# Output stage of a linear-attention block: numerators three output products ahead instead of four, and each residual add ahead of the division

## Chip, cores, metric

The kernel runs on one core of a Trainium2 chip. The metric is device time in microseconds (us), the median of several runs. All runs compared here are of the fast state; e11 is a single run, whose state is unknown, and serves for its profile alone. The kernel before takes 736.35 us (median of 6 runs, 735.11 to 737.95).

## The reference, cut to what matters

```
h  = x + attn(layernorm(x))          # S = 2048 tokens, D = 1024, 32 heads
h2 = h + reglu_mlp(layernorm(h))
# attn, after q, k, v and phi:
num = pq @ kv;  den = pq @ z + 1e-6
o = num / den                        # per token and head
attn = o @ wo
```

The change concerns the last two lines: the numerators, the division, the product with `wo` and the residual add, for 16 tiles of 128 tokens.

## The kernel before

Every operation is added to one plan with the buffers that it reads and writes. Each engine, and SyncE's DMA queue, works through its own list strictly in order. The functions of the output stage, cut to what matters:

```python
def a2_num(st):                      # N(st): 32 small matmuls into PSUM banks 0 to 3
    ...
def a2_div(st):                      # D(st): +1e-6, reciprocal, multiply, on VectorE
    ...
    dma_t(sl_to[kt], oT[:, kt, :, :], osb[:, k, :], ...)      # X(st): DMA transpose on SyncE's queue
def a4_mm(st):                       # O(st): 2 x 8 matmuls into a pair of banks (4,5 or 6,7)
    k = st % NOT                     # NOT = 4
    ...
def a4_h(st):                        # H(st): residual add on VectorE, frees the pair of banks
    ...
    if TPP <= st and st + NX2 < NST: # from tile 8 on: load x of tile st + 3
        load_x2(st + NX2)
    dma(sl_hs[hs], h_scr[...], hsb[:, hs, :], ...)            # W(st): store
    if st >= TPP: return
    ...                              # statistics of the second layer norm on ScalarE, GpSimd
def a4_norm(st):                     # L(st), then its DMA transpose Y(st), tiles 0 to 7
    ...
    dma_t(sl_tx[kx], hnT[...], xn[:, kx, :], ...)
```

The loop before (N, D and X of tiles 0 to 3 are done earlier, among the q products):

```python
LAG = NOT                            # 4
for t in range(NE, NST + LAG + 1):   # NE = 4
    if LAG <= t < NST + LAG:
        a4_mm(t - LAG)
    if t < NST:
        a2_num(t)
        a2_div(t)
    if LAG <= t < NST + LAG:
        a4_h(t - LAG)
    if LAG + 1 <= t < TPP + LAG + 1:
        a4_norm(t - LAG - 1)
    if t in (5, 7, 18, 19):
        load_w_next()                # 512 KB of feed-forward weights each
    ...                              # sums of weights on GpSimd, sums of tokens on VectorE
```

## Time and profile before

| | us |
|---|---|
| span of the profiled run | 734.9 |
| TensorE busy | 720.8 (98%) |
| from the end of O(0) to the end of O(15) | 57.6 |
| after O(15) | 503.7 |
| one step of the stage on TensorE: O 3.63, N 0.23 | 3.86 |

TensorE hardly ever waits, so the time is read from its waits and from what is about to become one. A line of the timeline gives start, length, engine, line of the kernel, operation, output<-input, and in brackets the idle time in front and what ended it. In names, RE<-RE is X, RH<-RXH is Y, h_scr<-RXH is W, RWG<-in_B_W_gate_dram and RWG<-in_B_W_up_dram are the weight loads; matmuls from RW,RE are O and from kvz,RAB are N.

### The profile page before, as it was taken

The page shows a single profiled execution, that of the slowest core. Times are in us where ns is not written, and L with a number is a line of the kernel's source. Part 1 is how long each engine was busy: PE and PEld are TensorE (multiplying, and loading weights), DVE is VectorE, ACT ScalarE, POOL GpSimd, SP SyncE. Part 2 cuts the span into 40 slices and gives each one's busy share as a digit, 9 for nine tenths or more (in the row PEclk, how much of TensorE's full clock was granted, in tenths as well). Part 3 has the DMA queues.
Part 4 walks back from the last instruction along what each step waited for, and adds up shares of the span by engine and source line. Part 5 has one row for each costly group of instructions (what it writes and reads, how often), then busy time and mean ns, then how long its engine had stood idle before and what let it go on. Part 6 is the DMA issues. An engine that isn't in the chain of part 4 may idle for free.

```text
span 734.9 us, 11505 instructions
## 1 busy us (share of the span) xinstructions
PE 720.8 (98%) x4253; PEld 363.2 (49%) x4311; DVE 561.6 (76%) x976; ACT 352.0 (48%) x614; POOL 103.7 (14%) x169
## 2 busy tenths in 40 slices
PE   8999999999999999999999999999999999999998
PEld 3444444344444444444444666754444444447766
DVE  7878877898775999898997769865757575667594
ACT  4877666764832456777754100135454544521000
POOL 1311100000450112132320003400000000000052
PEclk9999999999999999999999999999999999999999
DMA  9644154024999889888969999982323242327892
GB/s 313 202 91 83 29 142 157 3 30 75 214 228 260 234 258 272 241 243 256 300 198 305 318 247 336 311 263 79 101 71 109 63 116 58 100 92 245 246 314 87
DMA packets 191880, 133.93 MB, mean 182 GB/s; under 512 B 51664, under 2 KB 173776, under 8 KB 191824
## 3 DMA queue, kind: packets, MB, share of 16 engines
q1 hardware_dynamic: 191152, 132.54, 63.6%
q8 instruction: 34, 0.56, 0.3%
q10 hardware_dynamic: 672, 0.66, 0.3%
q14 instruction: 22, 0.18, 0.1%
HBM read 96.47 MB, written 25.17 MB: 166 GB/s over the span
## 4 chain that ended last, share of the span: by engine, by line
PE 82%; DVE 9%; DMA 3%; issue 2%; ACT 2%; SPq 1%; POOL 1%; POOLq 0%; DVEq 0%; ACTq 0%
PE ps L710 82%; DMA RW<-in_B_W_down_dram 1%; DVE RAB L796 1%; DVE RE L1171 1%; ACT RX L789 1%; DMA RX<-h_scr 1%; DVE st L724 1%; DMA RAB<-RXH 1%; DVE RX L793 1%; SPq L541 1%; DVE RX L1012 1%; DVE RO L1289 1%; POOL rstd L734 0%; DVE RW L906 0%; ACT ps L715 0%
## 5 line engine op out<-in xcount | busy, mean ns | idle before, releaser
L715 ACT ACTIVATE ps<-ps 128x512 f32<-128x512 f32 x172 | 100.1, 582 | 213.5 <-PE ps L710 162.0
L710 PE MATMUL ps<-RC,RO 128*128 128x512 f16 x672 | 154.3, 379 | 0.0
L710 PE MATMUL ps<-RH,RWG 128*128 128x512 bf16 x447 | 105.6, 379 | 0.1
L710 PEld LDWEIGHTS ps<-RC,RO 128*128 128x128 f16 x672 | 65.7, 98 | 79.5 <-ACT ps L715 0.5
L1345 DVE TENSOR_TENSOR RAB<-ps,RAB 128x512 bf16<-128x512 f32 x56 | 38.6, 689 | 71.9 <-PE ps L710 71.9
L710 PE MATMUL ps<-RC,RWG 128*128 128x512 f16 x320 | 76.8, 379 | 0.3 <-ACT ps L715 0.3
L1341 DVE TENSOR_TENSOR RE<-ps,RE 128x512 bf16<-128x512 f32 x112 | 74.2, 684 | 1.6 <-PE ps L710 0.7
L710 PEld LDWEIGHTS ps<-RH,RWG 128*128 128x128 bf16 x448 | 43.9, 98 | 52.6
L710 PE MATMUL ps<-RW,RAB 128*128 128x256 f16 (+3 forms) x412 | 66.8, 318 | 1.5 <-DVE RAB L1423 1.0
L1423 POOL TENSOR_TENSOR RE<-RE,RX 128x512 f32<-128x512 f32 x16 | 23.1, 1473 | 307.5 <-DMA RX<-h_scr 307.5
L715 ACT ACTIVATE RE<-RE 128x512 bf16<-128x512 bf16 x56 | 35.1, 627 | 65.0 <-DVE RE L1341 64.4
L710 PE MATMUL ps<-RH,RO 128*128 128x512 bf16 (+1 forms) x228 | 55.3, 379 | 3.0 <-DVE RE L1341 1.6
L710 PE MATMUL ps<-RW,RE 128*128 128x512 bf16 x243 | 56.6, 380 | 1.5 <-DVE RXH L1195 0.7
L710 PE MATMUL ps<-RAB 128*128 128x512 bf16 (+2 forms) x268 | 57.6, 351 | 0.4
L715 ACT ACTIVATE RE<-ps 128x512 f32<-128x512 f32 x64 | 37.6, 597 | 35.4 <-PE ps L710 35.0
L710 PEld LDWEIGHTS ps<-RW,RAB 128*128 128x128 bf16 (+1 forms) x414 | 40.4, 98 | 25.8 <-DVE RAB L1423 1.3
L710 PEld LDWEIGHTS ps<-RC,RWG 128*128 128x128 bf16 (+1 forms) x320 | 30.0, 98 | 40.2 <-ACT ps L715 6.2
L1289 DVE TENSOR_TENSOR RO<-RWG 128x1024 f16<-128x1024 bf16 x54 | 39.7, 736 | 4.7 <-DMA RWG<-in_B_W_up_dram 4.7
L1423 DVE TENSOR_TENSOR RE<-ps,RE 128x512 f32<-128x512 f32 x40 | 27.0, 687 | 18.9 <-PE ps L710 15.6
L715 ACT ACTIVATE RAB<-ps 128x512 bf16<-128x512 f32 x56 | 33.4, 596 | 14.7 <-PE ps L710 13.6
L710 PEld LDWEIGHTS ps<-RH,RO 128*128 128x128 f16 (+1 forms) x256 | 24.2, 98 | 31.8 <-DVE RE L1341 2.2
L710 PEld LDWEIGHTS ps<-RAB 128*128 128x128 bf16 (+1 forms) x274 | 26.3, 98 | 25.2 <-ACT RAB L856 1.1
(138 smaller groups left out, 994.0 us busy)
## 6 DMA issues: line engine op xcount, KB each, us to landing
RWG<-in_B_W_gate_dram SPq DMA_DIRECT2D x28, 512.0 KB, 5.0
RWG<-in_B_W_up_dram SPq DMA_DIRECT2D x28, 512.0 KB, 5.9
RW<-in_B_W_down_dram SPq DMA_DIRECT2D x14, 512.0 KB, 6.1
t_scr<-RW SPq DMA_DIRECT2D x14, 512.0 KB, 3.5
RE<-in_A_x_dram SPq DMA_DIRECT2D x23, 256.0 KB, 3.5
RW<-l_scr SPq DMA_DIRECT2D x13, 448.0 KB, 6.3
l_scr<-RX SPq DMA_DIRECT2D x7, 768.0 KB, 4.4
RW<-in_B_W_down_dram SPq DMA_DIRECT2D x12, 384.0 KB, 5.0
```

The costliest lines, as they stand in the source:

```text
L541: return PL.add(eng, lambda e: e.dma_start(dst_ap, src_ap), reads=reads, writes=writes, slot=slot, name=name)
L710: lambda e: e.matmul(out_ap, lhsT, rhs, start=start, stop=stop, skip_group_check=skip),
L715: PL.add("act", lambda e: e.activation(out=dst, in_=src, func=func), reads=reads, writes=writes, name=name)
L724: PL.add("dve", lambda e: e.bn_stats(out=st6[:, k, c * 6:(c + 1) * 6], in_=src_full[:, c * BCH:(c + 1) * BCH]), reads=[src_chunk_bufs[c]], ...
L789: PL.add("act", lambda e: e.activation(out=Et[:, k, :], in_=src, func=ACTF.Exp), reads=[src_buf], writes=[B_E[k]], name=name + "_exp")
L793: PL.add("dve", lambda e: e.tensor_scalar(out=Et[:, k, :], in0=Et[:, k, :], scalar1=1.0, scalar2=1e-6, op0=ALU.min, op1=ALU.add), reads=[] ...
L796: PL.add("dve", lambda e: e.scalar_tensor_tensor(out=dst_ap, in0=src, scalar=C1, in1=Et[:, k, :], op0=ALU.add, op1=ALU.max), reads=[src_bu ...
L1012: PL.add("dve", lambda e: e.tensor_tensor(out=s_, in0=p_, in1=s_, op=ALU.add), reads=[pb], writes=[sb_], name=name + "_add")
L1289: PL.add(eng, lambda e: e.tensor_tensor(out=tb(j, u), in0=f0(u), in1=f1(u), op=ALU.subtract), reads=[B_w[i + x] for x in r] + ([B_T[k + x] ...
L1341: PL.add("dve", lambda e: e.tensor_tensor(out=dst, in0=src, in1=ftmp[:, w, :], op=ALU.add), reads=[bsrc, B_s5[w]], writes=[bdst], name=name)
L1345: PL.add("dve", lambda e: e.tensor_tensor(out=dst, in0=a_, in1=b_, op=ALU.mult), reads=reads, writes=[wr], name=name)
L1423: PL.add(eng, lambda e: e.tensor_tensor(out=dst, in0=in0, in1=in1, op=op), reads=reads, writes=writes, name=name)
```

## The change

Its intent: D(4) kept VectorE from H(0), and O(2) waited for the banks that H(0) frees. The add goes ahead of the division in every step, and the numerators run three products ahead, so that no N stands between O(1) and O(2).

```diff
-        LAG = NOT
+        LEAD = 3
 ...
+        for t in range(NST + 1):
+            if t < NST:
+                a4_mm(t)
+                if t == 0:
+                    a2_num(NE)
+                    a4_h(0)
+                    a2_div(NE)
+                else:
+                    if t + LEAD > NE:
+                        if t + LEAD < NST:
+                            a2_num(t + LEAD)
+                        a4_h(t)
+                        if t + LEAD < NST:
+                            a2_div(t + LEAD)
+                    else:
+                        a4_h(t)
+            if 1 <= t <= TPP:
+                a4_norm(t - 1)
-            if t in (5, 7, 18, 19):
+            if t in (1, 3, 14, 15):
                 load_w_next()
 ...             # the other shifts by four are renamings: same place relative to O
```

More of the change, by code (lines that the diff above doesn't have):

```diff
@@ L1871, in bass_sequential_preLN__linear_attn_block__glu_gated_reglu__prompt_kernel, with a2 @@
         flush()
-        LAG = NOT
         pool_t = t_sums(0, "pool")
-        for t in range(NE, NST + LAG + 1):
-            if LAG <= t < NST + LAG:
-                a4_mm(t - LAG)
+        LEAD = 3
+        def a2(t):
             if t < NST:
@@ L1879, in bass_sequential_preLN__linear_attn_block__glu_gated_reglu__prompt_kernel @@
                 a2_div(t)
-            if LAG <= t < NST + LAG:
-                a4_h(t - LAG)
-            if LAG + 1 <= t < TPP + LAG + 1:
-                a4_norm(t - LAG - 1)
-            if t in (5, 7, 18, 19):
+        for t in range(NST + 1):
[17 more added lines that the diff above has]
+            if t in (1, 3, 14, 15):
                 load_w_next()
-            if t >= 9:
+            if t >= 5:
                 run(pool_t, 1)
-            if 15 <= t < 19:
-                s_sums()[t - 15]()
+            if 11 <= t < 15:
+                s_sums()[t - 11]()
+        run(pool_t, len(pool_t))
         load_w_next()
```

## The prediction

> **Names.** The output stage handles 16 token tiles. N(s) are the 32 numerator products of tile s, D(s) its division on VectorE (three instructions, lines 1166, 1169, 1171), X(s) the DMA transpose that puts the divided tile before TensorE, O(s) the 16 matmuls of the output product, H(s) the residual add (line 1195), W(s) the store of H(s), L(s) the second layer norm on ScalarE, Y(s) its DMA transpose (tiles 0 to 7 only). X, W, Y and all loads are issued by one queue, SyncE's, in program order.
>
> **What bounds the kernel now.** I read the page first: busy shares, then the chain of work that ended last.
>
> ```profile
> PE 720.8 (98%) x4253; PEld 363.2 (49%) x4311; DVE 561.6 (76%) x976; ACT 352.0 (48%) x614; POOL 103.7 (14%) x169
> ...
> PE 82%; DVE 9%; DMA 3%; issue 2%; ACT 2%; SPq 1%; POOL 1%; POOLq 0%; DVEq 0%; ACTq 0%
> ```
>
> TensorE is busy 720.8 of 734.9 us. So whatever the stage gains is time in which TensorE waits, and anything that makes it wait is added to the end. Next, the waits of TensorE: 1.6 us on line 1341, 1.4 on line 522, 1.0 on line 1423, and in the stage concerned one single wait of 0.7 us on H (line 1195). The timeline shows where it lies:
>
> ```profile
> 173.84 3.63 PE L710 MATMUL ps<-RW,RE 128*128 128x512 bf16 x15
> ...
> 176.06 1.23 DVE L1171 TENSOR_TENSOR RE<-ps,rden 128x1024 bf16<-128x1024 f32 x1
> 177.20 1.21 DVE L1195 TENSOR_TENSOR RXH<-ps,RC 128x1024 bf16<-128x1024 f32 x1
> 177.40 0.27 PEld L710 LDWEIGHTS ps<-kvz,RAB 32*128 32x128 bf16 x32 [0.42 <-DVE RE L1171]
> ...
> 178.47 1.90 PE L710 MATMUL ps<-RW,RE 128*128 128x512 bf16 x7 [0.70 <-DVE RXH L1195]
> ```
>
> O(1) runs at 173.84, N(5) at 177.40, then O(2) needs the two PSUM banks of O(0). H(0) frees them at 178.41, for VectorE did D(4) first. From O(2) on, the timeline has TensorE without a gap worth counting: O(3) starts at 182.33 and each next one 3.86 us later (3.63 for O, 0.23 for N), O(5) at 190.06, O(9) at 205.51, until O(15) ends at 231.17 and the feed-forward stage follows directly.
>
> The view that decides is SyncE's own timeline. Column two is how long the queue was occupied:
>
> ```profile
> 184.94 1.23 SPq L545 DMA_TRANSPOSE RH<-RXH  x1
> 186.21 0.58 SPq L541 DMA_DIRECT2D RWG<-in_B_W_gate_dram  x1
> 186.91 2.21 SPq L545 DMA_TRANSPOSE RE<-RE  x1
> 189.56 0.33 SPq L541 DMA_DIRECT2D h_scr<-RXH  x1
> 189.95 1.37 SPq L545 DMA_TRANSPOSE RH<-RXH  x1
> 191.44 2.07 SPq L545 DMA_TRANSPOSE RE<-RE  x1
> 193.56 0.58 SPq L541 DMA_DIRECT2D h_scr<-RXH  x1
> 194.19 1.29 SPq L545 DMA_TRANSPOSE RH<-RXH  x1
> 195.52 0.61 SPq L541 DMA_DIRECT2D RWG<-in_B_W_up_dram  x1
> 196.24 2.14 SPq L545 DMA_TRANSPOSE RE<-RE  x1
> 198.42 0.58 SPq L541 DMA_DIRECT2D h_scr<-RXH  x1
> 199.04 1.29 SPq L545 DMA_TRANSPOSE RH<-RXH  x1
> 200.45 1.27 SPq L545 DMA_TRANSPOSE RE<-RE  x1
> ```
>
> RE<-RE is X (here X(6) to X(9)), RH<-RXH is Y (Y(0) to Y(3)), h_scr is W. The queue is nearly solid. One tile costs it 3.2 us (1.27 + 0.58 + 1.29 and gaps) to 4.9 us (with a weight load and a 2.1 us X), against 3.86 us of TensorE. D(9) ended at 196.09, yet X(9) is issued at 200.45. Its landing, taken one by one from the view of line 545: X(6) 5.1 us, X(7) 4.1, X(8) 4.9, X(9) 4.8, X(10) 3.9, X(11) 3.1, X(12) 4.4. So X(8) lands at 196.24 + 4.9 = 201.1, and O(8) starts at 201.65; X(9) lands at 205.25, and O(9) starts at 205.51. The four tiles of lead, which look generous, are all used: 0.5 and 0.3 us are left.
>
> **What the Trainium skill says.** (1) "DMA: Bandwidth & Descriptors", section "Anatomy of one DMA": a DMA has a fixed part of about 2.0 us, most of it the receipt of the last write (given there for GpSimd's path), and semaphores are waited for on the issuing sequencer. Section "Latency and other measured facts" of that page has a transpose at 261 GB/s. My estimate from both: 2.0 + 256 KB/261 GB/s = 3.0 us. The trace agrees: X(0), issued with little else about, landed in 3.0 us; 3.1 to 5.1 under load. (2) "Perfetto Trace Analysis", section "What 'DMA-bound' means": a sequencer's track solid with DMA slices is a bound of its own. From 186.9 us on the trace agrees. (3) "VectorE: DVE Perf Modes", the section on the TRN2 errata: an f32 add of N columns takes (N+151)/0.96 ns, 1224 ns for 1024. Line 1195 has 1214 to 1219 ns here, line 1171 1225 ns. (4) "TensorE: Matmul & The Clock Gate", Part 1: the clock halves after an idle window of about 3.4 us. No wait below comes near that, and the mean granted clock here is 1.000.
>
> **The change part by part.** Instruction counts don't change on any engine. Positions of the weight loads, GpSimd sums and S sums relative to O(t) don't change either. Two things do.
>
> *H(0) before D(4).* VectorE is free at 175.4 us. H(0) runs to 176.6, D(4) to 178.5, H(1) from 178.4 to 179.6. O(2) starts straight after O(1), at 177.47. Removed: the 0.70 us wait. D(4) is 1.1 us later; X(4) then lands by about 182 and O(4) wants it at 185.2: beside other work. N(5) moves behind O(2), which costs nothing in sum. Gain 0.7 us.
>
> *Three tiles of lead, add before division in each step.* Per step the queue's order was Y(t-2), X(t+4), W(t), Y(t-1); it becomes W(t), X(t+3), Y(t-1). X(s) thus stands one W more, one Y and in some steps a load further back, 2.5 to 3.1 us. Also D(t+3) waits behind H(t). It ends about 0.1 + 1.13 + 0.23 + 0.46 + 1.23 = 3.2 us after O(t) (the starts of 1195, 1166, 1169, 1171 follow each other so in the trace); now it is 2.4 us.
>
> Step 2, the first with the shorter lead, times from the durations above:
> - O(2) ends at 181.1, D(5) at 184.3.
> - L(0) ended 3.56 us after H(1) (184.92 against 181.36). With H(1) at 179.6 it ends at 183.2. Y(0) goes out there; the next X went out 1.97 us after it (184.94 to 186.91, a weight load between), plus 0.6 for W(2) now between: X(5) at 185.8.
> - It lands after 3.9 us (X(5) before) to 5.1 us (X(6), at this place in the queue): 189.7 to 190.9.
> - O(5) is due at 177.47 + 3 x 3.86 = 189.05. TensorE waits 0.7 to 1.9 us; I take 1.7.
>
> Then, with the waits entered: X(5) holds the queue 2.2 us, Y(1) 1.3, W(3) 0.6: X(6) at 190.0, landed 194.1 to 194.9, O(6) due 194.6: about nothing. X(6) 2.1, Y(2) 1.3, load 0.7, W(4) 0.6: X(7) at 194.7, landed 198.8 to 199.6, O(7) due 198.5: 0.3 to 1.1, I take 0.7. X(7) 2.1, Y(3) 1.3, W(5) 0.7: X(8) at 198.8, landed near 203.4, O(8) due 203.1: 0.3. From there the loop closes over three tiles: O ends, D 3.2 us later, 0.3 to issue, about 4.1 to land, 0.2 to start, 3.63 for O: 11.4 us, against 3 x 3.86 = 11.6. It is in balance, so I give 0.3 us in all for a late landing. Sum: 1.7 + 0.7 + 0.3 + 0.3 = 3.0 us of new waits, less 0.7: the stage 2.3 us longer. All later work starts from O(15)'s end on TensorE, so it shifts by as much.
>
> **Rivals.**
> - *The intended gain and no more.* If X lands in 3.0 to 3.4 us, the wait at O(5) is 0.2 us or less and later ones vanish: 735.5 to 735.8 us. For it: later X land in 3.1 and 3.2 us, and waits of TensorE thin out the DMA load. Against: the measured landings at this place, 3.9 to 5.1.
> - *A longer jam.* X at 4.8 us or more each time: each turn of the loop (11.4 + 0.7) exceeds 11.6 by 0.5 us, some three more turns: 740 us. For it: DMA engines about fully busy from 190 to 226 us. Against: X(10), X(11), X(13) came in 3.9 us or less.
> - *VectorE or the banks become the wait.* H(t) now comes first, so banks come free 2 us sooner; N(t+3) needs D(t+2), done 0.6 us before. Nothing new: about 736.
> - *Clock.* Waits under 2 us leave it at 1.0.
>
> **Range and chances.** 736.2 + 2.3 = 738.5; allowing some weight to the first rival I say 738.0. Low end 735.2 (gain kept, and the runs of before spread over 735.1 to 738.0), high end 740.9 (the jam). 2% is 14.7 us, a quarter of this stage of 61 us: none of this reaches it. Faster 0.005, same 0.985, slower 0.01.
>
> **What would show it.** Right: no wait before O(2); TensorE waits of 0.5 to 2 us for a DMA into RE (X) just before O(5), and one or two smaller ones by O(8); X(5) issued near 185.8; O(15) ending 1 to 4 us later than 231.17. Wrong: O(5) starts at about 189 without a wait (then X landed in 3.2 us or less, or Y(0) left the queue sooner), and O(15) ends near 230.4.

## The result

The changed kernel takes 740.2 us (median of 6 runs, 739.66 to 744.01). Its ratio to before is 1.0069, with a 95% interval from 1.0043 to 1.0095. In a later job it was 740.17 us and 1.0051 (1.0036 to 1.0066). A ratio is the mean time of one kernel's fast runs over that of the other's of the same rounds, so it is not quite the ratio of the medians; the record lists two more fast runs of the changed kernel in that job, 744.70 and 740.93 us, and 1.0069 fits the mean of all eight. The loss is 3.9 us where 1.8 had been predicted.

The page of the changed kernel, first profile, busy shares and chain of work that ended last:

```profile
PE 727.0 (98%) x4311; PEld 364.5 (49%) x4311; DVE 561.7 (76%) x976; ACT 352.0 (47%) x614; POOL 104.1 (14%) x169
...
PE 87%; DMA 4%; DVE 3%; ACT 2%; SPq 1%; issue 1%; POOL 1%; POOLq 0%; ACTq 0%; DVEq 0%
PE ps L710 86%; DMA RE<-RE 2%; DMA RE<-l_scr 1%; DMA RE<-in_A_x_dram 1%; SPq L545 1%; ACT RX L789 1%; DMA RAB<-RXH 1%; POOL RX L1423 1%; DVE RO L1289 1%; SPq L541 1%; ACT ps L715 0%; ACT RXH L748 0%; DMA RX<-h_scr 0%; POOL RE L1423 0%; DVE RAB L1345 0%
```

X (DMA RE<-RE) is now on the chain with 2% of the span. This profile fell on the slowest of the six runs (744.01 us), though: its windows show why it must not be taken for the typical one. The columns are the stretch, its length, each engine's busy time (and instructions), the granted clock, the DMA share and GB/s:

```profile
5.00:10.00 5.00, 2.75 (x15) 1.15 (x14) 3.00 (x8) 0.99 (x2) 1.11 (x2) 0.87 1.07 371
10.00:15.00 5.00, 5.00 (x32) 2.59 (x31) 4.14 (x11) 1.91 (x5) 1.09 (x2) 0.79 1.10 355
```

The clock was low from 5 to 15 us, before anything that was changed; O(0) started 2 us later than in the kernel before. So I took a second profile of the same kernel (run e5 below), with a full clock in that part. What TensorE waited for there, in the order reason: sum in us, times, longest:

```profile
PE ps L710 <- DMA RE<-RE: 4.4, 3, 2.4
PE ps L710 <- POOL RXH L522: 1.4, 1, 1.4
PE ps L710 <- DVE RE L1341: 1.2, 1, 1.2
```

In the first profile the first of these lines reads 5.5 us, also three times. The kernel before has no such line. TensorE's timeline of the second profile shows where:

```profile
173.47 7.08 PE L710 MATMUL ps<-RW,RE 128*128 128x512 bf16 x31
...
190.93 1.37 PE L710 MATMUL ps<-RW,RE 128*128 128x512 bf16 x4 [2.35 <-DMA RE<-RE]
192.53 3.72 PE L710 MATMUL ps<-RW,RE 128*128 128x512 bf16 x11 [0.22 <-issue]
...
201.05 3.63 PE L710 MATMUL ps<-RW,RE 128*128 128x512 bf16 x15 [0.64 <-DMA RE<-RE]
...
221.89 3.40 PE L710 MATMUL ps<-RW,RE 128*128 128x512 bf16 x15 [1.46 <-DMA RE<-RE]
```

The first line is O(1) and O(2) in one: the old wait is gone. O(5), O(7) and O(12) now wait for their transposes. A product has 16 matmuls, and the trace has lost the record of some: where a line of 15 is 3.40 us long instead of 3.63, the first is missing, and the wait in brackets is too long by 0.23 us, here and in the runs below (at O(12) it was 1.23). And O(5), 3.63 us long elsewhere, takes 5.3 us here, for the granted clock (third number from the end) was 0.69 from 190 to 194 us:

```profile
190.00:194.00 4.00, 2.85 (x8) 1.22 (x10) 1.30 (x2) 3.12 (x5) 1.32 (x4) 0.69 1.18 253
194.00:198.00 4.00, 3.95 (x47) 1.67 (x46) 1.62 (x3) 0.34 (x1) 0.00 (x0) 0.89 0.94 229
```

SyncE's queue ahead of those tiles, same profile:

```profile
182.87 1.23 SPq L545 DMA_TRANSPOSE RH<-RXH  x1
184.16 0.57 SPq L541 DMA_DIRECT2D RWG<-in_B_W_gate_dram  x1
184.77 0.64 SPq L541 DMA_DIRECT2D h_scr<-RXH  x1
185.53 1.59 SPq L545 DMA_TRANSPOSE RE<-RE  x1
...
192.71 0.64 SPq L541 DMA_DIRECT2D RWG<-in_B_W_up_dram  x1
193.40 0.63 SPq L541 DMA_DIRECT2D h_scr<-RXH  x1
194.14 2.41 SPq L545 DMA_TRANSPOSE RE<-RE  x1
```

X(5) goes out at 185.53 behind Y(0), a weight load and W(2), X(7) at 194.14 behind the other load and W(4). They land 5.4 and 6.9 us after that (view of line 545, one transpose at a time); X(6) and X(8), with no weight load just in front, land after 3.8 us each.

The stage, from the end of O(0) to the end of O(15), takes 57.6 and 57.7 us in two profiles of before, 64.1 and 62.8 us in the two of the changed kernel.

### The profile page after: what moved, and what is told of

Same layout as the page of the kernel before. It is cut to its first block, busy times and chain, and to the rows that moved or that the text cites. A ratio compares the mean times of both kernels' runs of the same rounds, so it can differ in the third digit from the quotient of the medians.

```text
span 742.3 us, 11564 instructions
## 1 busy us (share of the span) xinstructions
PE 727.0 (98%) x4311; PEld 364.5 (49%) x4311; DVE 561.7 (76%) x976; ACT 352.0 (47%) x614; POOL 104.1 (14%) x169
## 4 chain that ended last, share of the span: by engine, by line
PE 87%; DMA 4%; DVE 3%; ACT 2%; SPq 1%; issue 1%; POOL 1%; POOLq 0%; ACTq 0%; DVEq 0%
PE ps L710 86%; DMA RE<-RE 2%; DMA RE<-l_scr 1%; DMA RE<-in_A_x_dram 1%; SPq L545 1%; ACT RX L789 1%; DMA RAB<-RXH 1%; POOL RX L1423 1%; DVE RO L1289 1%; SPq L541 1%; ACT ps L715 0%; ACT RXH L748 0%; DMA RX<-h_scr 0%; POOL RE L1423 0%; DVE RAB L1345 0%
## 5 line engine op out<-in xcount | busy, mean ns | idle before, releaser
L710 PE MATMUL ps<-RW,RE 128*128 128x512 bf16 x256 | 59.2, 387 | 5.5 <-DMA RE<-RE 5.5
L710 PE MATMUL ps<-RH,RO 128*128 128x512 bf16 (+1 forms) x256 | 61.2, 379 | 1.2 <-DVE RE L1341 1.2
L710 PEld LDWEIGHTS ps<-RW,RE 128*128 128x128 bf16 x256 | 24.5, 99 | 34.7 <-DMA RE<-RE 5.8
```

What stands on the lines that cost most here:

```text
L710: lambda e: e.matmul(out_ap, lhsT, rhs, start=start, stop=stop, skip_group_check=skip),
```

## The experiments

The theory: with a lead of three, X reaches TensorE late, above all behind a weight load in SyncE's queue. Rivals: the residual add ahead of the division delays the division and so X; the mere place at the start of the stage; the clock. "Wait" is TensorE's. All results were correct.

**e1: the first part alone.** Lead four, H(0) ahead of D(4).

```diff
             if t < NST:
                 a2_num(t)
+                if t == NE:
+                    a4_h(t - LAG)
                 a2_div(t)
-            if LAG <= t < NST + LAG:
+            if LAG < t < NST + LAG:
```

> The kernel before with one part of the change alone: H(0) ahead of D(4), lead of four tiles kept. Theory (the loss comes from transposes X that reach TensorE late because the lead is three): no wait of TensorE before O(2), none for X anywhere, 0.7 us faster than before, about 735.6 us. Rival (the residual add ahead of the division delays D and so X): X(4) later by 1.1 us, but it had over 3 us, so no wait here either; this run alone does not refute the rival, it prices the first part.

Measured: 737.26 us, ratio 1.0012 (0.9994 to 1.003). No gain, so the expectation failed. TensorE's timeline:

```profile
178.68 0.37 PE L710 MATMUL ps<-kvz,RAB 32*128 32x33 bf16 x32 [1.13 <-DVE RE L1171]
178.99 3.63 PE L710 MATMUL ps<-RW,RE 128*128 128x512 bf16 x15
```

O(2) starts at 178.99, no sooner than before (178.47). With a lead of four N(5) still stands in front of O(2), and it waits for D(4), which now comes second. The old wait has only changed its name, and O(9) waits 0.3 us more (0.53 in the list, less the 0.23 of a missing record); the list names VectorE, but X(9) landed at 206.5 us, just before O(9) began. The gain needs both parts of the change.

**e2: lead four, add first in every step.**

```diff
             if t < NST:
                 a2_num(t)
-                a2_div(t)
             if LAG <= t < NST + LAG:
                 a4_h(t - LAG)
+            if t < NST:
+                a2_div(t)
```

> Lead of four kept, but in every step the residual add H(t) ahead of the division D(t+4). Theory (lead): X(s) moves back by one store W in the queue, 0.6 us; O(8) and O(9), which had 0.5 and 0.3 us, may wait some tenths; total within 0.7 us of before, 735.5 to 737. Rival (the order of add and division is the cause): most of the loss of 3.9 us appears here, 739 us or more.

Measured: 736.38 us, ratio 0.9999 (0.9982 to 1.0016). Waits: 1.1 us of N(5) for D(4), 0.4 us of O(9) for X(9). As the theory had it; the order of add and division is not what costs 3.9 us.

**e3: lead three, division first from step 2 on.**

```diff
                         if t + LEAD < NST:
                             a2_num(t + LEAD)
-                        a4_h(t)
-                        if t + LEAD < NST:
                             a2_div(t + LEAD)
+                        a4_h(t)
```

> The changed kernel (lead of three) with the division ahead of the residual add again from step 2 on. Theory (lead): X(s) gains only one store W in the queue, 0.6 us, waits at O(5) and O(7) shrink from 2.4 and 1.9 us to about 1.8 and 1.3; 738.5 to 739.5 us. Rival (order): the waits vanish, 735.5 to 736.5 us.

Measured: 741.84 us, ratio 1.0069 (1.0054 to 1.0084). TensorE's wait for X in the list (sum, times, longest):

```profile
PE ps L710 <- DMA RE<-RE: 5.8, 3, 2.6
```

The rival of the order falls, but the theory's number is missed too: waits of 1.4 us at O(5), 2.6 at O(7) and 1.8 at O(12), no smaller in sum than in the changed kernel. X(5) and X(7) had one store fewer in front and still landed in 5.0 and 6.6 us. The stage took 62.6 us, as in the changed kernel (62.8 in e5); that this run is longer lies mostly after O(15), where its profile has a wait of 1.4 us for a load from the scratch tensor `l_scr` that e5 lacks.

**e4: lead three, the two weight loads ahead of the stage.**

```diff
         pool_t = t_sums(0, "pool")
+        load_w_next()
+        load_w_next()
 ...
-            if t in (1, 3, 14, 15):
+            if t in (14, 15):
```

> The changed kernel, with the two weight loads of steps 1 and 3 issued ahead of the output stage instead, so that no 512 KB load stands in the queue before X(5) and X(7). If those loads are what made X(5) and X(7) land in 5.4 and 6.5 us: they land in about 4 us and are issued 0.6 us earlier, the waits fall to about 0.4 us at O(5) and none at O(7), total 736 to 737 us. If the shorter lead is too short whatever the loads do: waits of over 1 us stay at O(5) or later, total 739 us or more.

Measured: 736.53 us, ratio 1.0002 (0.9984 to 1.002). X(5) is issued at 185.57 and lands in 3.8 us, X(7) in 4.8. TensorE's timeline, O(7) and O(12):

```profile
197.50 3.63 PE L710 MATMUL ps<-RW,RE 128*128 128x512 bf16 x15 [0.31 <-DMA RE<-RE]
...
218.49 3.40 PE L710 MATMUL ps<-RW,RE 128*128 128x512 bf16 x15 [1.61 <-DMA RE<-RE]
```

These are all its waits for X in the list; O(5) starts 0.17 us later than straight after its N (188.92 + 0.30, against 189.39). Moving two loads undoes nearly the whole loss. The wait at O(12) is not theirs: X(12) goes out behind Y(7), a 256 KB load of x and W(9), 213.33 against 208.75 for X(11), and lands in 4.9 us.

**e5: the changed kernel again.** No edit.

> The changed kernel once more, unedited, for a second profile: the first fell on the slowest of its runs, with a granted clock of 0.79 to 0.87 from 5 to 15 us and of 0.66 in O(7). Theory (late X are the cause, the clock is not): clock at 1.0 or nearly, span near 738.5 us, and still three waits for X of 4.5 us or more in sum, at O(5), O(7) and O(12). Rival (the clock makes a good part): with the clock at 1.0 the loss against before falls below 2.5 us.

Measured: 740.17 us, ratio 1.0051. Waits for X 4.4 us at O(5), O(7) and O(12). The clock was at 1.0 but for 190 to 198 us. Of its four runs, two had a mean clock of 1.000 and took 740.57 and 740.38 us, two 0.997 and 0.998 and took 739.97 and 739.56 us: the loss does not follow the clock.

**e6: the two loads from ScalarE's queue.**

```diff
-                load_w_next()
+                load_w_next("act" if t < 14 else "sp")
 ...             # load_w_next hands the engine on to dma(...)
```

> The changed kernel, the two weight loads at the same steps but issued by ScalarE's queue instead of SyncE's. If X(5) and X(7) are slow because the load's descriptors stand in front of theirs in the same queue: they land in about 4 us, waits at O(5) and O(7) of 0.4 us or less, total about 737 us as in the run with early loads. If it is the mere traffic of 512 KB on the shared DMA engines: X(5) and X(7) still land in 5 to 6.5 us, less 0.6 us for the load's issue time, waits of 1 to 2 us each stay, total 739 us or more.

Measured: 737.55 us, ratio 1.0014 (0.9999 to 1.0029). X(5) and X(7) land in 4.1 and 4.2 us; waits 0.4 us at O(5), 0.7 at O(6), 1.4 at O(12). It looks like the first expectation, but the test is not clean: on ScalarE's queue the loads went out at 181.55 and 188.25 us instead of 184.16 and 192.71, so they were further ahead of X in time as well. Whether it was their place in the queue or their traffic is left open for X(5) and X(7). One case of the same run says that traffic counts: X(6) went out at 189.55 us, 1.30 us behind a load that stood in the other queue, and landed in 4.9 us, against 3.8 in e5 and 3.6 in e4, where no load was that near.

**e7: the loads two steps after the sensitive place.**

```diff
-            if t in (1, 3, 14, 15):
+            if t in (5, 7, 14, 15):
 ...
-            if t >= 5:
+            if t >= 9:
```

> The changed kernel with the two weight loads moved from steps 1 and 3 to steps 5 and 7 (GpSimd's sums of those weights from step 9). Theory (a load in front of X makes it late): the waits move along, O(5) and O(7) wait 0.3 us or less, O(9) and O(11) 1 to 2.5 us each, total again near 740 us. Rival (the start of the stage is what makes X late, the loads only stand there): O(5) and O(7) wait as before, O(9) and O(11) don't.

Measured: 739.84 us, ratio 1.0054 (1.0037 to 1.007). TensorE's timeline, O(5), O(7), O(9), O(11), O(12):

```profile
189.31 3.63 PE L710 MATMUL ps<-RW,RE 128*128 128x512 bf16 x15 [0.20 <-DMA RE<-RE]
...
197.31 3.63 PE L710 MATMUL ps<-RW,RE 128*128 128x512 bf16 x15 [0.21 <-DMA RE<-RE]
...
205.63 3.63 PE L710 MATMUL ps<-RW,RE 128*128 128x512 bf16 x15 [0.54 <-DMA RE<-RE]
...
215.30 3.63 PE L710 MATMUL ps<-RW,RE 128*128 128x512 bf16 x16 [1.87 <-DMA RE<-RE]
220.47 3.40 PE L710 MATMUL ps<-RW,RE 128*128 128x512 bf16 x15 [1.24 <-DMA RE<-RE]
```

The waits moved with the loads, to O(9) and O(11), if less at O(9) than I had expected. The rival of the place falls.

**e8: numerators in the middle of the output product.** A lead of three and a half, loads in place.

```diff
-        def a4_mm(st):
+        def a4_mm(st, mid=None):
 ...
             for nt in range(ND2):
+                if nt == 1 and mid is not None:
+                    mid()
 ...
-                a4_mm(t)
+                a4_mm(t, (lambda: a2_num(t + LEAD)) if NE < t + LEAD < NST else None)
 ...             # and the division ahead of the add, as in e3
```

> The changed kernel with the numerators of tile t+3 in the middle of the output product O(t) instead of behind it, the division ahead of the add, loads in place: a lead of three and a half. D(t+3) ends 2.7 us earlier than in the changed kernel and X(t+3) stands before W(t). Theory (queue order and the load in front set X's time, not the division's end): X(5) and X(7) still go out behind Y, load and land in 5 to 6.5 us; waits of over 3 us in sum, 738.5 to 741 us. Rival (the late division sets it): waits below 1 us in sum, 736 to 737 us.

Measured: 738.71 us, ratio 1.0034 (1.0016 to 1.0052). X(5) lands in 5.3 us and X(7) in 7.2; waits of 1.6 us before O(5) and 2.5 before O(7), none of note at O(12). TensorE's timeline, the first half of O(5):

```profile
190.80 1.89 PE L710 MATMUL ps<-RW,RE 128*128 128x512 bf16 x8 [1.62 <-DVE RXH L1197]
```

The list names an add, H(4), which ended at 190.76 us. O(5) needs the banks of H(3), free since 186.90, and X(5), which landed at 185.36 + 5.3 = 190.7: so I read it as a wait for X. An earlier division does not help the two tiles behind a load, and it does help tile 12.

**e9: e8 with the loads early, as in e4.**

> A version meant to keep the gain without the loss: numerators in the middle of the output product (lead of three and a half), division ahead of the add, and the two weight loads ahead of the stage. Theory (a load in front of X, together with the short lead, is the loss): no wait before O(2), waits for X of 0.3 us or less in sum, also at O(12); the stage 0.7 to 1.0 us shorter than before, 735.3 to 736.0 us, at most 0.1% faster. Rival (the short lead alone is too short): waits of over 1 us in sum, 737 us or more.

Measured: 734.92 us (734.26 to 736.0, 6 runs) against 736.85 us (11 runs), ratio 0.998 (0.9965 to 0.9994): a version a little faster than both kernels. TensorE has no wait for X at all:

```profile
174.06 5.35 PE L710 MATMUL ps<-RW,RE 128*128 128x512 bf16 x23
179.88 3.40 PE L710 MATMUL ps<-RW,RE 128*128 128x512 bf16 x15 [0.16 <-issue]
```

These are O(1) and half of O(2), then N(5), then the next two halves. The stage takes 56.9 us.

**e10: the kernel before with the loads early** (the edit of e4, lead four).

> The kernel before (lead of four, its order) with the two weight loads ahead of the stage: the fourth cell of lead three or four by loads in place or early. Theory (with a lead of four the loads were hidden already, by 0.3 us at the tightest): nothing to gain, the wait before O(2) stays at about 0.7 us, the margins at O(8) and O(9) grow to over 1 us; 736.0 to 736.8 us, ratio within 0.1% of 1. Rival (the loads cost time by themselves, whatever the lead): 1 us or more faster than before.

Measured: 735.75 us, ratio 0.9992 (0.9977 to 1.0007). The wait before O(2) stays, none for X. TensorE's timeline, O(2):

```profile
178.58 3.63 PE L710 MATMUL ps<-RW,RE 128*128 128x512 bf16 x15 [0.71 <-DVE RXH L1195]
```

With a lead of four the loads were hidden already: taking them away gains nothing that these rounds can tell from zero. Lead and loads hurt only together:

| median us (before of the same job) | loads in place | loads early |
|---|---|---|
| lead four | 736.35 | 735.75 (736.85) |
| lead three | 740.17 (736.38) | 736.53 (736.43) |

**e11: the kernel before again.**

> The kernel before, unedited, for a second profile of the time after O(15), which took 503.7 us in the first profile of before and 501.7 us in the second of the changed kernel. If that difference is the run's and not the change's, this profile shows another value between 501.5 and 505.5; if the change shortens that part, it shows 503.7 again within 0.3.

Measured: one run, 735.78 us; after O(15) 502.4 us. So that part varies from run to run. X(6), X(7) and X(8) landed in 5.5, 4.8 and 5.0 us, where the first profile of before had 5.1, 4.1 and 4.9.

**e12: TensorE kept busy in the waits.**

```diff
+            for _ in range(8 if st in (5, 7) else 0):
+                mm(bank(b, NW), ident[:], wo[:, 0, 0:NW], True, True, [B_ident, B_wo[0]], B_bank[b], "busy_%d" % st)
```

> The changed kernel with eight useless matmuls (1.7 us) ahead of O(5) and of O(7), where TensorE waits for X anyway; their results are overwritten. If the clock that fell after the waits of 1.9 and 2.4 us costs time: no window of the stage below full clock, O(5) and O(7) at 3.63 us each, and the total 0.5 to 1.5 us below the changed kernel's 740.2 us. If the clock's fall only stands in place of later waiting, or where the waits are shorter than 1.7 us and the matmuls themselves delay O: 740 us or more.

Measured: 740.27 us, ratio 1.0056 (1.0044 to 1.0069). The mean clock was 1.000 in all six runs. TensorE's timeline, the idle matmuls and O(5), then the same at O(7):

```profile
189.32 1.90 PE L710 MATMUL ps<-RW,ident 128*128 128x512 bf16 x8
191.86 3.63 PE L710 MATMUL ps<-RW,RE 128*128 128x512 bf16 x16 [0.64 <-DMA RE<-RE]
...
199.58 1.90 PE L710 MATMUL ps<-RW,ident 128*128 128x512 bf16 x8
201.67 3.63 PE L710 MATMUL ps<-RW,RE 128*128 128x512 bf16 x16 [0.19 <-DMA RE<-RE]
```

The useless matmuls fill 1.9 us of each wait, the rest stays, and the time is the same as with the clock falling. O(7) starts when X(7) lands, in either case. So the fall of the clock is real, and without it the loss is the same: it costs nothing that shows in the total. In a single run it may cost: the first profile of the changed kernel, where it fell in O(7) and no late transpose stood right behind, has a stage of 64.1 us, against 62.8 (e5, the fall in O(5)) and 62.2 (e12, none).

## Why the prediction was right or wrong

- **What bounds the kernel; no wait before O(2).** Right for the change as a whole, and no wait for VectorE or the banks came up in the stage. But the prediction booked the 0.7 us, and with it the move of N(5) behind O(2), under "H(0) before D(4)". That move comes from the lead of three, and e1 shows that without it the first part gains nothing.
- **Place and time of the new waits.** Right. X(5) was expected at 185.8 us and went out at 185.53 (e5, where O(0) had ended 0.4 us sooner than before); Y(0) was expected at 183.2 and went out at 182.87. O(5) and O(7) wait, O(6) doesn't. The waits at a tile behind each load moved with the loads in e7 and all but vanished in e4.
- **The step that failed: how long X takes to land, and so how long TensorE waits for it.** The queue, the place and the kind of wait were right; the terms were too small. Their sum was 3.0 us of new waits, and the first profile has 5.5 (2.40, 1.87 and 1.24). The working had 3.9 to 5.1 us for X(5) and 4.1 to 4.9 for X(7), values that transposes had at that place in the kernel before. Measured were 5.4 us, and 6.5 (first profile) and 6.9 us. The term for O(5), 1.7 us, was 2.35 to 2.40; that for O(7), 0.7 us, was 1.87 in the first profile, 0.64 in the second (O(5) took 1.7 us longer there at the low clock; X(7) landed at 194.14 + 6.9 = 201.0, just when O(7) started, so without that O(7) would have waited 2.3), and 2.1 in e12 with the clock kept up (1.90 filled, 0.19 left). The 5.4 us of X(5) is no news of the change: X(6), behind the same load, landed in 5.1 to 5.5 us in the four profiles with a lead of four and the loads in place (before, e1, e2, e11), and the prediction had one of them. The transpose behind the second load is: X(8) took 4.9 to 5.3 us in those four, X(7) 6.5 to 7.2 in the five with the shorter lead and that load in its place (the changed kernel twice, e3, e8, e12). Why is not settled; the store in front of X(7) isn't the reason (e3), and the shorter lead alone isn't either, for in e7, with the loads later, X(11) landed within 5.2 us behind the same load.
- **"0.3 us in all" for the later tiles.** Too small: 1.24 us at O(12) in the first profile and 1.23 in the second (the 1.46 shown, less the missing record). I had counted Y, W and X but not that from step 8 the loads of x join the queue while Y(7) still goes out. The wait at O(8) that I had put at 0.3 us did not come.
- **"Waits under 2 us leave the clock at 1.0."** Wrong: in the first profile the clock fell to 0.66 in a window of 4 us after a wait of 1.87 us, in the second to 0.69 after one of 2.35. As a cause of the loss it is refuted by e12.
- **All later work shifts by as much.** Not quite. The stage grew by 5.1 to 6.5 us, the kernel by 3.9. After O(15) before took 503.7 and 502.4 us, the changed kernel 502.3 and 501.7. Something near 1 us seems to come back there, but it is not shown: that part takes 502.4 to 505.6 us in the five profiles with a lead of four and 501.7 to 503.8 in the nine with a shorter one. A wait of TensorE for a load from the scratch tensor `l_scr` makes part of the spread and comes with either lead (2.2 us in e1, 1.1 in e10, 1.4 in e3).
- **The mark of 738.0 us.** The sum was 738.5; I had moved it towards the rival of short landings, which was the wrong side. The rival of a longer jam was nearer in size, if not by its mechanism: late were two tiles behind loads and one behind the loads of x, not every turn of the loop.

## What to carry to other kernels

A lead in tiles is worth only what the in-order DMA queue leaves of it: take the landing time of the last transfer that arrives before it is needed, and if 0.3 us are left, don't shorten the lead without first moving the large loads to another time (e4, e9). When a wait is removed by reordering, look for the instruction that stands between, for the wait may only pass to it (e1). And before a fallen clock is blamed, fill the wait and see whether the time changes (e12).

## What the Trainium skill lacked or had wrong

- "TensorE: Matmul & The Clock Gate", Part 1: the page has the clock fall after an idle window of about 3.4 us. Here it fell to 0.69 in a window of 4 us that began in a wait of 2.35 us (e5), and to 0.66 after one of 1.87 us (first profile), some 8 us after the end of another of 2.40; in e3 waits of 1.4 and 2.6 us left it at 1.00.
- "DMA: Bandwidth & Descriptors": I found no page that says how much a DMA transpose is held up by a load in front of it in the same queue. 256 KB landed in 3.0 us alone, 3.8 and 4.8 (X(5), X(7) of e4) among stores and transposes, 5.4 and 6.5 to 6.9 behind a load of 512 KB and a store.
- "Perfetto Trace Analysis": the section on what "DMA-bound" means calls the sequencer's window descriptor generation. The page's own section on the HWDGE instruction counts a wait for the lock and the push of semaphores in as well, but neither has a time. A transpose of the same size held SyncE for 1.23 us when little was under way and for 2.41 us behind a load (X(7) of e5); which part grew, no run shows.
